# Eleven exponential tiles, a product in place and reordered ScalarE copies in an attention and feedforward kernel

## The chip, the cores and the metric

The kernel runs on one core of a Trainium2 chip. The metric is the device time of one execution in microseconds (us); lower is better. A core has five engines that run their own instruction queues in order: TensorE (PE in the profile, with its weight loads apart as PEld), VectorE (DVE), ScalarE (ACT), GpSimd (POOL) and SyncE (SP), which issues all the DMAs here. Semaphores make one engine wait for another.

## The reference

For x of 2048 tokens by 512, in float32:

```python
xn = layernorm(x)                                  # no gain, no bias
q, k, v = split(xn @ wqkv)                         # 32 heads of 16
p = softmax(q @ k.T * 16 ** -0.5)                  # 2048 x 2048 for each head
s = concat(p @ v) @ wo
h = (xn @ w_gate) * (xn @ w_up)                    # 2048 x 1792
g = silu(h @ w_down)
out = x + s * g
```

## The kernel before

**Attention in units and rounds.** The 32 heads are taken in 8 groups of four, and the queries in 4 chunks of 512: 32 units. A unit has 16 rounds of 128 keys, so there are 512 rounds, numbered `n` in the main loop (L863). In a round, for each of the four heads j, `expo` (L611) lets TensorE compute a transposed 128 x 512 score tile `t` with the maxima folded in as two more rows, and ScalarE takes the exponential of it into an SBUF tile `e`. Between them `score` (L587) computes, 21 rounds ahead (`LEAD`), a score tile `s` whose row maxima VectorE reduces (`mx`, L594); `maxima` (L596) turns these into the rows that a later unit subtracts.

**The value block.** In every even round, after its four `expo`, `values` (L848) first runs what has been put into `before_values`, and then `block` (L622): TensorE multiplies V with the eight `e` tiles of the two rounds before, four heads side by side in the columns of the array, into one PSUM bank `pv`. ScalarE copies it to `part` (L639; the first of a unit straight to `acc`, L634), and GpSimd adds `part` to `acc` (L640, recorded as L65, as is everything that GpSimd and SyncE issue through the helper there). `finish` (L642) normalises a finished unit with two VectorE transposes and stores it to DRAM.

**Rings.** `t` and `pv` share three PSUM banks (tag `st`) in the order of use: of the nine tiles in two rounds, `pv` comes last, the first `t` after it takes the bank that the third `t` of the even round had, the next `t` that of the fourth, and the third `t` that of `pv` itself. `s` has three banks, the tag `misc` of the filler two. The `e` tiles are a ring of ten (`EBUFS`), `part` a ring of two. When the third exponential of an even round is issued, eight tiles wait for the block and two more hold the round's first exponentials.

**The filler.** Between the heads' steps, in three of the four gaps of a round (`GAPS`), `Filler.part` emits matmuls of other work so that TensorE has something between scores: at first the projections of the next heads (`proj_pair`, 13 pairs), then the feedforward (`ffn`, L364), then the output (`ending`, L468). All of it is done in float32r with each operand split into a high and a low half and three terms. `pair` (L268) computes two results at once in the upper and the lower 64 rows of the array, in two halves; after the first half ScalarE reads one element of it (`look`, L289). A pair of the feedforward gives gate and up; ScalarE copies the gate out of PSUM to `g` (L392, one tile), VectorE multiplies it with up into `h` (L349, one tile), and GpSimd splits `h` into `hh` and `hl`. The copy stands in ScalarE's queue where the pair ends, the product waits in `before_values`. Down-projected results `y` are written or added up by `add` (L408), also in `before_values`. A finished chunk's `silu` (L352) gives four steps of tanh on ScalarE and two operations on GpSimd; `later` takes one step in the rounds with `kt % 4 == 2` (L887), after the round's fourth exponential. Weights are loaded whole and split by GpSimd some steps after (`soon`, L124).

**The end.** `ending` multiplies the heads' outputs, loaded back and split by `o_split` (L422), with `wo` (loaded and split in one go in L398), and `end` (L451) makes `x + s * g`: VectorE multiplies `z` in PSUM with the silu into SBUF (L458), and GpSimd, or late in the kernel VectorE (L459), adds x. For every second tile of the last chunk VectorE multiplies in PSUM (L454) and adds from there (L455).

**Order.** The program order is kept on TensorE, ScalarE and VectorE (`ORDERED`, L48). GpSimd's and SyncE's instructions are put in order by the framework's scheduler after the first 18 rounds, so that a change elsewhere can move them.

Of the kernel before, what the change touches and what calls it, by code (L numbers as in the profile page):

```python
# [11 lines left out]
F32 = mybir.dt.float32  # L12
F32R = mybir.dt.float32r
# [20 lines left out]
GAPS = [(0, 1, 2), (1, 2, 3)]  # L34
SLOTS = 24 * (NC * (NG // 2 - 1) + 1) + 36 * NF * NC
SPLIT_ROUNDS = 4
EBUFS = 10
PBUFS = 2
HBUFS = 2
QBUFS = 2  # L40
FINAL_AT = 8
# [9 lines left out]
def body(ctx, tc, x, wqkv, wo, wg, wu, wd, out):  # L51
# [23 lines left out]
    def dma(dst, src):  # L75
        sync.dma_start(dst, src)
# [72 lines left out]
    def etile():  # L149
        return ep.tile([P, 512], F32, name="e", bufs=EBUFS)  # L150

    def parts():
        return ep.tile([P, 512], F32, name="part", bufs=PBUFS)

    qkv = ExitStack()
    qp = qkv.enter_context(tc.tile_pool(name="qkv", bufs=1))
# [75 lines left out]
    def split_rows(raw, hi, lo):  # L232
        pool.tensor_copy(hi, raw)
        pool.tensor_tensor(lo, raw, hi, op=OP.subtract)
# [110 lines left out]

    later = []

    def product(h, u, g, hi, lo):
        nc.vector.tensor_tensor(h, u, g, op=OP.mult)  # L349
        split_rows(h, hi, lo)  # L350

    def silu(fp, c, y):  # L352
        for t in range(4):
# [12 lines left out]
    def ffn(nxt):  # L366
        fp = fst["fp"]
        for c in range(NC):
            if c == 0:
                fh, fl = xh[0], xl[0]  # L370
            else:
                fh, fl = [keep.tile([P, ND, 512], F32R, name=n) for n in ("fh", "fl")]
                dmar(fh, XD[c][0])
                dmar(fl, XD[c][1])
            y = fp.tile([P, 4, D], F32, name="y")
            for ti, fs in enumerate(THIRDS):
                hh = fp.tile([P, 5, 512], F32R, name="hh")
                hl = fp.tile([P, 5, 512], F32R, name="hl")
                dh = fp.tile([P, 5, D], F32R, name="dh")
                dl = fp.tile([P, 5, D], F32R, name="dl")  # L380
                for i, f in enumerate(fs):
                    ws = nxt
                    if not (c == NC - 1 and f == NF - 1):
                        nxt = gu_weights((f + 1) % NF)
                    raw = fp.tile([P, D], F32, name="wdr", bufs=2)
                    dma(raw, wd[f * P:(f + 1) * P])
                    soon(8, lambda raw=raw, i=i, dh=dh, dl=dl: split_rows(raw, dh[:, i], dl[:, i]))
                    outs = []
                    yield from pair(outs, [("misc", f"{n}{c}_{f}") for n in "gu"], [terms(lambda d: wh[:, d], lambda d: wl[:, d],
                                                 lambda d: fh[:, d], lambda d: fl[:, d], ND) for wh, wl in ws])  # L390
                    g = fp.tile([P, 512], F32, name="g", bufs=1)
                    nc.scalar.activation(g, outs[0], AF.Copy)  # L392
                    h = fp.tile([P, 512], F32, name="h", bufs=1)
                    before_values.append(lambda h=h, u=outs[1], g=g, hi=hh[:, i], lo=hl[:, i]: product(h, u, g, hi, lo))
                if c == NC - 1 and fs[-1] == NF - 1:
                    fst["y"] = y
                    fst["w"] = [keep.tile([P, ND, D], F32R, name=n) for n in ("fh", "fl")]
                    for d in range(ND):  # L398
                        raw = fp.tile([P, D], F32, name="wdr", bufs=2)
                        dma(raw, wo[d * P:(d + 1) * P])  # L400
                        split_rows(raw, *[t[:, d] for t in fst["w"]])
                for t in range(0, 4, 2):
                    outs = []
                    yield from pair(outs, [("misc", f"y{c}_{ti}_{u}") for u in (t, t + 1)], [terms(lambda i: hh[:, i, u * P:(u + 1) * P],
                                                 lambda i: hl[:, i, u * P:(u + 1) * P],
                                                 lambda i: dh[:, i], lambda i: dl[:, i], len(fs)) for u in (t, t + 1)])
                    for n, o in enumerate(outs):
                        def add(o=o, y=y[:, t + n], first=ti == 0, n=n):  # L408
                            if first and n:
                                nc.vector.tensor_copy(y, o)  # L410
                            elif first:
                                nc.scalar.activation(y, o, AF.Copy)
                            else:
                                nc.vector.tensor_tensor(y, o, y, op=OP.add)  # L414
                        before_values.append(add)
            later.append(silu(fp, c, y))


# [3 lines left out]
    def o_split(c, tiles):  # L422

        for d, (oh, ol) in enumerate(tiles):
            heads = 8 if c < NC - 1 or d < ND - 1 else 4
            n = heads * DH
            raw = (wtile(("w1r", "w0r")[d]).rearrange("p d q -> p (d q)") if d < 2 else
                   fst["fp"].tile([P, D], F32, name="wdr", bufs=2))
            dma(raw[:n], OD[c][8 * d:8 * d + heads, 0:DH])
            pool.tensor_copy(oh[:n], raw[:n])  # L430
            pool.tensor_tensor(ol[:n], raw[:n], oh[:n], op=OP.subtract)
        ops[c] = now[0], tiles

    def small_tiles():
# [15 lines left out]

    def end(c, t, o, yt, xt):  # L451
        tt = 4 * c + t
        if t % 2 and c == NC - 1:
            nc.vector.tensor_tensor(o, o, yt, op=OP.mult)  # L454
            nc.vector.tensor_tensor(yt, o, xt, op=OP.add)  # L455
        else:
            late = now[0] >= NU * 16 - LEAD and c < NC - 1
            nc.vector.tensor_tensor(yt, o, yt, op=OP.mult)  # L458
            (nc.vector if late else pool).tensor_tensor(yt, yt, xt, op=OP.add)  # L459
        dma(out[tt * P:(tt + 1) * P], yt)  # L460

    def o_terms(c, t):
# [80 lines left out]

    def last_heads():
        fp = fst["fp"]
        th = fp.tile([P, 512], F32, name="g", bufs=1).bitcast(F32R)
        tl = fp.tile([P, 512], F32, name="h", bufs=1).bitcast(F32R)
        nc.scalar.activation(th, fst["tn"], AF.Copy)
        nc.vector.tensor_tensor(tl, fst["tn"], th, op=OP.subtract)
        fst["t"] = th, tl  # L550
# [71 lines left out]
    def block(todo):  # L622

        i = todo[0][0]
        g = i // NC
        o = psum("st", f"pv{i}")
        for n, (_, kt, es) in enumerate(todo):
            for j in range(4):
                h0 = (4 * g + j) * VW
                nc.tensor.matmul(o[32 * j:32 * j + 32], V[:, kt, h0:h0 + 32], es[j],  # L630
                                 start=n == 0, stop=n == len(todo) - 1)
        if todo[0][1] == 0:
            sums[i] = keep.tile([P, 512], F32, name="acc", bufs=2)
            nc.scalar.activation(sums[i], o, AF.Copy)  # L634
        elif i >= NU - 2 and kt >= NT - 2:
            nc.vector.tensor_tensor(sums[i], o, sums[i], op=OP.add)
        else:
            part = parts()
            nc.scalar.activation(part, o, AF.Copy)  # L639
            pool.tensor_tensor(sums[i], sums[i], part, op=OP.add)  # L640

# [29 lines left out]
    def early():  # L671
# [5 lines left out]
        for which in (1, 0):  # L677
            wraw.append(wtile(f"w{which}r"))
            dma(wraw[-1], wqkv[:, which * D:which * D + P].rearrange("(d p) f -> p d f", p=P))
        norm["raws"] = raws = [etile() if d < 2 else parts() for d in range(ND)]  # L680
        for d in range(ND):
            dma(raws[d], wqkv[d * P:(d + 1) * P, 2 * D:])
        for tt in range(4, NT):
# [115 lines left out]
    def step_small(q):  # L799
        if q and next(q[0], 1):  # L800
            q.pop(0)
# [57 lines left out]
    with tc.manual_schedule(engines=ORDERED):  # L859
# [3 lines left out]
        for n in range(NU * 16):  # L863
            now[0] = n
            Tied.on = n < 18
            i, kt = divmod(n, 16)
            g, c = divmod(i, NC)
            si, sr = divmod(n + LEAD, 16)
            if kt == 8 and i + 2 < NU:
                load_q(i + 2)  # L870
            if kt == 0 and g + 1 < NG and c == 1:
                load_k(g + 1)
            es = []
            for j in range(4):
                es.append(expo(i, kt, j))
                if si < NU:
                    score(si, sr, j ^ 1)
                step()
                if j == 1:
                    prepare()  # L880
                if n and j in GAPS[n % 2]:
                    if fil.done:
                        fil = Filler(ending(), lambda n: 2)
                    fil.part(n % 2 and j == 1)
            if sr == 15 and si < NU:
                maxima(si, 8 if si < NU - 1 else 4)
            if kt % 4 == 2:  # L887
                step_small(later)
            if n == 0:
                run(fst["v"])  # L890
            elif n % 2 == 0 or n == NU * 16 - 1:
                values()
            prev.append((i, kt, es))
# [27 lines left out]
```

## Time and profile before

| | us |
|---|---|
| median of 3 runs | 1832.85 (1831.91 to 1835.38) |
| the profiled execution's own time | 1833.15 |
| its span, first to last instruction | 1831.4 |
| TensorE busy | 1784.9 |
| VectorE busy | 1479.7 |
| ScalarE busy | 1297.9 |
| GpSimd busy | 884.3 |

The mean granted TensorE clock was 0.995 of full speed. A line of the profile's groups gives the source line, the engine, the operation with its tiles (written `out<-in`), the shapes and the count; then the busy time, the mean duration of one in ns, and the engine's idle time ahead of them with what ended it. A line of waits gives who waited for whom, the sum in us, how often, and the longest. A line of a timeline gives the start in us, the duration, and the instruction, with the idle time ahead of it in brackets. A granted TensorE clock of 0.5 means half speed. Matmul ends are modelled, so starts are the better measure.

### The profile page before, as it was taken

The page shows a single profiled execution, that of the slowest core. Times are in us where ns is not written, and L with a number is a line of the kernel's source. Part 1 is how long each engine was busy: PE and PEld are TensorE (multiplying, and loading weights), DVE is VectorE, ACT ScalarE, POOL GpSimd, SP SyncE. Part 2 cuts the span into 40 slices and gives each one's busy share as a digit, 9 for nine tenths or more (in the row PEclk, how much of TensorE's full clock was granted, in tenths as well). Part 3 has the DMA queues.
Part 4 walks back from the last instruction along what each step waited for, and adds up shares of the span by engine and source line. Part 5 has one row for each costly group of instructions (what it writes and reads, how often), then busy time and mean ns, then how long its engine had stood idle before and what let it go on. Part 6 is the DMA issues. An engine that isn't in the chain of part 4 may idle for free.

```text
span 1831.4 us, 35270 instructions
## 1 busy us (share of the span) xinstructions
PE 1784.9 (97%) x13578; PEld 1074.6 (59%) x13578; DVE 1479.7 (81%) x2441; ACT 1297.9 (71%) x2575; POOL 884.3 (48%) x919
## 2 busy tenths in 40 slices
PE   9999999999999999999999999999999999999998
PEld 6655555555655555556656555655655556556554
DVE  6878888788888888888888888888888888888832
ACT  6257777677777777777777777777777777777765
POOL 5214444743644546455354653553546445355562
PEclk9999999999999999999999999999999999999999
DMA  5317523511231122311024210411135111011341
GB/s 200 98 44 219 219 97 124 146 39 39 62 74 51 61 77 67 74 50 51 28 62 111 73 56 28 97 50 39 42 96 113 40 51 51 27 53 55 115 136 69
DMA packets 117235, 145.79 MB, mean 80 GB/s; under 512 B 12620, under 2 KB 74060, under 8 KB 114380
## 3 DMA queue, kind: packets, MB, share of 16 engines
q1 hardware_dynamic: 117068, 143.55, 26.7%
q8 instruction: 106, 1.74, 0.4%
q14 instruction: 61, 0.50, 0.1%
HBM read 95.94 MB, written 47.45 MB: 78 GB/s over the span
## 4 chain that ended last, share of the span: by engine, by line
PE 88%; ACT 5%; issue 3%; POOL 2%; DMA 1%; DVE 1%; SPq 0%; ACTq 0%; POOLq 0%; DVEq 0%
PE pv L630 22%; PE t L617 20%; PE s L592 10%; PE g L285 5%; PE u L285 5%; PE y L281 4%; PE y L285 4%; PE g L281 4%; PE u L281 3%; ACT e L619 2%; PE p L285 2%; PE v L262 2%; PE p L281 2%; ACT g L392 1%; PE z L285 1%
## 5 line engine op out<-in xcount | busy, mean ns | idle before, releaser
L594 DVE TENSOR_REDUCE mx<-s 128x1 f32<-128x512 f32 x2048 | 1305.1, 685 | 209.3 <-PE s L592 163.2
L619 ACT ACTIVATE e<-t 128x512 f32<-128x512 f32 x2048 | 1121.9, 611 | 461.6 <-PE pv L630 410.8
L617 PE MATMUL t<-qs,ks 50*128 50x512 f32 x2048 | 846.9, 425 | 25.6 <-ACT e L619 24.6
L592 PE MATMUL s<-ks,qs 48*128 48x512 f32 x2048 | 835.1, 428 | 3.3 <-DVE mx L594 2.5
L617 PEld LDWEIGHTS t<-qs,ks 50*128 50x128 f32 x2048 | 377.9, 185 | 370.3 <-ACT e L619 282.6
L65 POOL TENSOR_TENSOR acc<-acc,part 128x512 f32<-128x512 f32 x222 | 286.4, 1290 | 465.4 <-ACT part L639 465.3
L630 PE MATMUL pv<-e,V 128*32 128x512 f32 x4096 | 492.5, 598 | 0.0
L592 PEld LDWEIGHTS s<-ks,qs 48*128 48x128 f32 x2048 | 368.8, 184 | 31.2 <-issue 6.1
L630 PEld LDWEIGHTS pv<-e,V 128*32 128x32 f32 x4096 | 107.1, 109 | 240.8 <-issue 216.3
L639 ACT ACTIVATE part<-pv 128x512 f32<-128x512 f32 x222 | 134.2, 604 | 0.8 <-POOL acc L65 0.7
L285 PE MATMUL u<-fh,w0h 64*128 64x512 f32 x224 | 90.3, 403 | 1.8 <-DVE h L349 1.8
L349 DVE TENSOR_TENSOR h<-u,g 128x512 f32<-128x512 f32 x56 | 38.7, 692 | 65.4 <-ACT g L392 62.1
L285 PE MATMUL y<-dh,hh 64*128 64x512 f32 x224 | 91.1, 407 | 0.1
L281 PE MATMUL u<-fh,w0h 64*128 64x512 f32 x224 | 90.6, 405 | 0.0
L285 PE MATMUL g<-fh,w1h 64*128 64x512 f32 x224 | 90.4, 404 | 0.0
L65 POOL CAST w0h<-w0r 128x512 fp32r<-128x512 f32 x60 | 36.6, 610 | 110.9 <-PE u L281 82.7
L281 PE MATMUL y<-dh,hh 64*128 64x512 f32 x224 | 89.3, 399 | 0.7 <-DVE y L414 0.7
L285 PE MATMUL u<-fl,w0h 64*128 64x512 f32 x224 | 88.5, 395 | 0.0
L285 PE MATMUL u<-fh,w0l 64*128 64x512 f32 x224 | 88.4, 395 | 0.0
L281 PE MATMUL g<-fh,w1h 64*128 64x512 f32 x224 | 88.4, 395 | 0.0
L281 PE MATMUL g<-fh,w1l 64*128 64x512 f32 x224 | 88.4, 394 | 0.0
L281 PE MATMUL g<-fl,w1h 64*128 64x512 f32 x224 | 88.2, 394 | 0.0
(261 smaller groups left out, 3093.6 us busy)
## 6 DMA issues: line engine op xcount, KB each, us to landing
w0r<-in_wu_dram SPq DMA_DIRECT2D x56, 256.0 KB
w1r<-in_wg_dram SPq DMA_DIRECT2D x56, 256.0 KB
wdr<-in_wd_dram SPq DMA_DIRECT2D x56, 256.0 KB
qs<-QD SPq DMA_DIRECT2D x64, 192.0 KB
ks<-KD SPq DMA_DIRECT2D x12, 768.0 KB
KD<-hl SPq DMA_DIRECT2D x16, 512.0 KB
QD<-hl SPq DMA_DIRECT2D x16, 512.0 KB
OD<-acc SPq DMA_DIRECT2D x31, 256.0 KB
```

Source lines behind the costliest of these rows:

```text
L65: got = getattr(self.engine, name)(*args, **kw)
L262: nc.tensor.matmul(o, l(d), r(d), start=k == d == 0, stop=k == 2 and d == ND - 1)
L281: nc.tensor.matmul(outs[k], l[LOWER], r[LOWER], start=k == 0 and n == 0, stop=(stop or k == 0) and n == len(low) - 1, skip_group_check=k == 1)
L285: nc.tensor.matmul(outs[1 - k], l[UPPER], r[UPPER], start=k == 0 and m == 0, stop=(stop or k == 0) and m == len(high) - 1, skip_group_chec ...
L349: nc.vector.tensor_tensor(h, u, g, op=OP.mult)
L392: nc.scalar.activation(g, outs[0], AF.Copy)
L592: nc.tensor.matmul(o, QS[i][b:b + KB, pr, t * P:(t + 1) * P], k[b:b + KB, pr, kc * 512:(kc + 1) * 512], start=True, stop=True)
L594: nc.vector.tensor_reduce(MX[i][:, j, t, kc:kc + 1], o, axis=AX.X, op=OP.max)
L617: nc.tensor.matmul(o, k[b:b + KR, pr, kt * P:(kt + 1) * P], QS[i][b:b + KR, pr], start=True, stop=True)
L619: nc.scalar.activation(e, o, AF.Exp, scale=DH ** -0.5)
L630: nc.tensor.matmul(o[32 * j:32 * j + 32], V[:, kt, h0:h0 + 32], es[j], start=n == 0, stop=n == len(todo) - 1)
L639: nc.scalar.activation(part, o, AF.Copy)
```

## The change

Six edits: the `e` tiles become eleven, and `part` has one buffer of its own and, once the feedforward's pool is open, a second one in that pool (`part2`), used in turn; the product of gate and up is written over the gate's copy `g`, of which there are now two, and `h` is gone; the `silu` step moves from behind the round's fourth exponential to ahead of it, and the first of the first third's two `y` copies is issued where its pair ends and no longer in `before_values`; the loads and splits of `wo` and the splits in `o_split` are spread over later steps; outputs of the last 21 rounds' range are multiplied in PSUM and added from there on VectorE. TensorE's order stays the same.

```diff
-EBUFS = 10
-PBUFS = 2
+EBUFS = 11
...
-    def parts():
-        return ep.tile([P, 512], F32, name="part", bufs=PBUFS)
+    turn = [0]
+
+    def part_tile():
+
+        turn[0] ^= 1
+        if turn[0] and "fp" in fst:
+            return fst["fp"].tile([P, 512], F32, name="part2", bufs=1)
+        return ep.tile([P, 512], F32, name="part", bufs=1)
...
-    def product(h, u, g, hi, lo):
-        nc.vector.tensor_tensor(h, u, g, op=OP.mult)
-        split_rows(h, hi, lo)
+    def product(u, g, hi, lo):
+        nc.vector.tensor_tensor(g, u, g, op=OP.mult)
+        split_rows(g, hi, lo)
...
-                    g = fp.tile([P, 512], F32, name="g", bufs=1)
+                    g = fp.tile([P, 512], F32, name="g", bufs=2)
                     nc.scalar.activation(g, outs[0], AF.Copy)
-                    h = fp.tile([P, 512], F32, name="h", bufs=1)
-                    before_values.append(lambda h=h, u=outs[1], g=g, hi=hh[:, i], lo=hl[:, i]: product(h, u, g, hi, lo))
+                    before_values.append(lambda u=outs[1], g=g, hi=hh[:, i], lo=hl[:, i]: product(u, g, hi, lo))
...
                     for d in range(ND):
-                        raw = fp.tile([P, D], F32, name="wdr", bufs=2)
-                        dma(raw, wo[d * P:(d + 1) * P])
-                        split_rows(raw, *[t[:, d] for t in fst["w"]])
+                        def wo_split(d=d, w=fst["w"]):
+                            raw = fp.tile([P, D], F32, name="wdr", bufs=2)
+                            dma(raw, wo[d * P:(d + 1) * P])
+                            soon(4, lambda: split_rows(raw, *[t[:, d] for t in w]))
+                        soon(5 * d + 4, wo_split)
...
-                        before_values.append(add)
+                        if ti == n == 0:
+                            add()
+                        else:
+                            before_values.append(add)
...
             dma(raw[:n], OD[c][8 * d:8 * d + heads, 0:DH])
-            pool.tensor_copy(oh[:n], raw[:n])
-            pool.tensor_tensor(ol[:n], raw[:n], oh[:n], op=OP.subtract)
+            soon(4 + 3 * d, lambda raw=raw[:n], oh=oh[:n], ol=ol[:n]: split_rows(raw, oh, ol))
...
-        if t % 2 and c == NC - 1:
+        if now[0] >= NU * 16 - LEAD and (t % 2 or c < NC - 1):
             nc.vector.tensor_tensor(o, o, yt, op=OP.mult)
             nc.vector.tensor_tensor(yt, o, xt, op=OP.add)
         else:
-            late = now[0] >= NU * 16 - LEAD and c < NC - 1
             nc.vector.tensor_tensor(yt, o, yt, op=OP.mult)
-            (nc.vector if late else pool).tensor_tensor(yt, yt, xt, op=OP.add)
+            pool.tensor_tensor(yt, yt, xt, op=OP.add)
...
-            part = parts()
+            part = part_tile()
...
-        norm["raws"] = raws = [etile() if d < 2 else parts() for d in range(ND)]
+        norm["raws"] = raws = [etile() if d < 3 else part_tile() for d in range(ND)]
...
             for j in range(4):
+                if j == 3 and kt % 4 == 2:
+                    step_small(later)
                 es.append(expo(i, kt, j))
...
-            if kt % 4 == 2:
-                step_small(later)
```

More of the change, by code (lines that the diff above doesn't have):

```diff
@@ L545, in last_heads @@
         fp = fst["fp"]
-        th = fp.tile([P, 512], F32, name="g", bufs=1).bitcast(F32R)
-        tl = fp.tile([P, 512], F32, name="h", bufs=1).bitcast(F32R)
+        th, tl = [fp.tile([P, 512], F32, name="g", bufs=2).bitcast(F32R) for _ in range(2)]
         nc.scalar.activation(th, fst["tn"], AF.Copy)
```

## The prediction

> **What bounds the kernel now.** I read the page first: span and busy times, then the chain, then the two costliest groups.
>
> ```profile
> span 1831.4 us, 35270 instructions
> ...
> PE 1784.9 (97%) x13578; PEld 1074.6 (59%) x13578; DVE 1479.7 (81%) x2441; ACT 1297.9 (71%) x2575; POOL 884.3 (48%) x919
> ...
> PE 88%; ACT 5%; issue 3%; POOL 2%; DMA 1%; DVE 1%; SPq 0%; ACTq 0%; POOLq 0%; DVEq 0%
> ...
> L594 DVE TENSOR_REDUCE mx<-s 128x1 f32<-128x512 f32 x2048 | 1305.1, 685 | 209.3 <-PE s L592 163.2
> L619 ACT ACTIVATE e<-t 128x512 f32<-128x512 f32 x2048 | 1121.9, 611 | 461.6 <-PE pv L630 410.8
> ```
>
> TensorE carries the chain, and looks full. But a matmul's record runs on while its weights are late, so busy time is no proof; the waits are. They are the second view:
>
> ```profile
> ACT e L619 <- PE pv L630: 410.8, 255, 1.9
> PEld t L617 <- ACT e L619: 282.6, 610, 0.8
> DVE h L349 <- ACT g L392: 62.1, 55, 1.5
> PEld t L617 <- ACT look L289: 44.4, 53, 0.8
> PEld t L617 <- ACT part L639: 15.9, 64, 0.6
> ```
>
> In 255 of the 256 value blocks ScalarE idles until the block's matmuls give it a free `e` tile, and behind that the weight load of a score matmul waits for an exponential. The third view, timelines of TensorE and ScalarE around blocks, gives the price. A plain block:
>
> ```profile
> 916.21 1.92 PE L630 MATMUL pv<-e,V 128*32 128x512 f32 x16
> 918.06 0.49 PE L617 MATMUL t<-qs,ks 50*128 50x512 f32 x1
> ...
> 918.43 0.50 PE L617 MATMUL t<-qs,ks 50*128 50x512 f32 x1
> ...
> 918.76 0.39 PE L285 MATMUL u<-fh,w0h 64*128 64x512 f32 x1
> ```
> ```profile
> 917.29 1.09 ACT L619 ACTIVATE e<-t 128x512 f32<-128x512 f32 x2 [1.54 <-PE pv L630]
> 918.26 0.61 ACT L634 ACTIVATE acc<-pv 128x512 f32<-128x512 f32 x1
> ```
>
> The block begins at 916.21. Only at 917.29, 1.08 later, can the third and fourth exponentials of the round run. The first `t` behind the block uses the third's bank and is in time; the second `t` uses the fourth's, and comes at 918.43, 0.37 behind the first; the next pair follows 0.33 later. And a block where ScalarE has a copy to make between the two exponentials:
>
> ```profile
> 1430.23 0.49 PE L617 MATMUL t<-qs,ks 50*128 50x512 f32 x1
> ...
> 1431.08 0.50 PE L617 MATMUL t<-qs,ks 50*128 50x512 f32 x1 [0.35 <-ACT e L619]
> ...
> 1431.42 0.39 PE L285 MATMUL u<-fh,w0h 64*128 64x512 f32 x1
> ...
> 1431.66 0.39 PE L285 MATMUL u<-fl,w0h 64*128 64x512 f32 x1
> ```
> ```profile
> 1429.45 0.60 ACT L619 ACTIVATE e<-t 128x512 f32<-128x512 f32 x1 [1.30 <-PE pv L630]
> 1429.95 0.59 ACT L392 ACTIVATE g<-g 128x512 f32<-128x512 f32 x1
> 1430.42 0.60 ACT L619 ACTIVATE e<-t 128x512 f32<-128x512 f32 x1
> 1430.90 0.62 ACT L639 ACTIVATE part<-pv 128x512 f32<-128x512 f32 x1
> ```
>
> Here 0.85 lies between the two `t`. The rhythm: a pair behind one whose weights were loaded late follows at 0.34 (1431.08 to 1431.42), any other at 0.24 (1431.42 to 1431.66).
>
> [...]
>
> **The change part by part.** *Eleven tiles.* When the third exponential of an even round is issued, eight tiles wait for the block and two hold the round's first exponentials. With eleven it finds one free; only the fourth waits for the block, 1.08 into it. At 0.60 it ends 1.68 into it. The first `t` comes at 1.85 (918.06 less 916.21), so the second `t` can have its weights loaded behind it, at 0.34, with the next pair at 0.24. Copies and `look` fall before the fourth exponential, into the wait. Which blocks gain what: the copies are counted by
>
> ```profile
> L392 ACT ACTIVATE g<-g 128x512 f32<-128x512 f32 x56 | 33.2, 592 | 0.0
> L318 ACT ACTIVATE qr<-p 128x512 f32<-128x512 f32 x13 | 7.7, 592 | 0.0
> ```
>
> - Copy blocks, 56 + 13 = 69: (0.85 - 0.34) + (0.34 - 0.24) = 0.61 each, 42.1.
> - `look` blocks, 53 by the waits' row: one of them is
>
> ```profile
> 1437.58 0.49 PE L617 MATMUL t<-qs,ks 50*128 50x512 f32 x1
> ...
> 1437.97 0.49 PE L617 MATMUL t<-qs,ks 50*128 50x512 f32 x1
> ...
> 1438.31 0.40 PE L285 MATMUL g<-fh,w1h 64*128 64x512 f32 x1
> ```
>
>   (0.39 - 0.34) + (0.34 - 0.24) = 0.15, together 8.0.
> - Plain blocks, 255 - 69 - 53 = 133: (0.37 - 0.34) + (0.33 - 0.24) = 0.12. Where TensorE later waits for the exponentials that queue behind the block's copy, only what the copy gains counts: it starts at 918.26 and the block's matmuls end at 918.13 (916.21 + 1.92), so 0.13 at most less a signal's delay. I take 0.09 to 0.12, 0.10: 13.3 (12.0 to 16.0).
>
> Sum 63.4. What hides the third exponential is ScalarE's idle 1.3 to 1.5 ahead of the block's release; if that cover were gone the gain would be too.
>
> *Product in place, two `g`.* VectorE's 692 ns product is the same work. Once, the old `h` cost TensorE time: VectorE could not overwrite it until GpSimd had read it.
>
> ```profile
> 356.28 0.39 PE L281 MATMUL g<-fh,w1h 64*128 64x512 f32 x1
> 358.46 0.59 PE L285 MATMUL u<-fh,w0h 64*128 64x512 f32 x1 [1.80 <-DVE h L349]
> ```
> ```profile
> 357.00:362.00 5.00, 3.54 (x18) 2.79 (x20) 3.27 (x5) 2.27 (x5) 5.00 (x6) 0.67 0.03 7
> ```
>
> The gap is 2.18 where 0.24 is normal, 1.94. Behind it the granted clock was 0.67 in a 5 us stretch: with only full and half speed, 0.33 x 2 x 5 = 3.3 us at half, which costs 1.7. Now VectorE writes into the tile that ScalarE just filled and waits for no reader. 3.6 gained. The `g` copy waits for the split of two products back instead; that is far off.
>
> *The silu step ahead of the fourth exponential.* Tanh used to run between the fourth exponential and the copy of `pv`, so that the third `t` waited for that copy:
>
> ```profile
> 678.58 0.50 PE L617 MATMUL t<-qs,ks 50*128 50x512 f32 x1 [0.21 <-ACT part L639]
> ```
>
> The row of waits for `part` sums to 15.9 in 64 cases, but these overlap other work. Sixteen steps at most, 0.2 to 0.4 each: 3 to 6; I take 4, and let the `y` copies, which save one wait and may delay an exponential, cost 1 of it. 3.
>
> *`part`: a cost.* In the first stage `part` has one buffer. A copy must then wait for GpSimd's addition of the one before. 27 copies lie there (the row below, for 0 to 320 us), and one pair of them overlaps:
>
> ```profile
> L639 ACT ACTIVATE part<-pv 128x512 f32<-128x512 f32 x27 | 16.3, 605 | 0.0
> ```
> ```profile
> 195.84 0.61 ACT L639 ACTIVATE part<-pv 128x512 f32<-128x512 f32 x1
> ```
> ```profile
> 197.75 1.28 POOL L65 TENSOR_TENSOR acc<-acc,part 128x512 f32<-128x512 f32 x1
> ```
>
> The addition of the part before ends at 199.03, held up by weight splits on GpSimd, so this copy waits 3.19. Queued behind it on ScalarE are all the next exponentials, and the third `t` waits for its bank: TensorE stops about 3.2. A shorter stop, the 2.18 above, was followed by 3.3 us of half clock; so 1.7 more, and -4.9. If the clock stays up it is -3.2; if a second copy meets the same, -9.8.
>
> [...]
>
> *The late multiply in PSUM.* Before, the addition took two SBUF operands, and one of them ran beside GpSimd's additions:
>
> ```profile
> 1751.86 3.94 DVE L459 TENSOR_TENSOR hh<-hh 128x512 f32<-128x512 f32 x1
> 1755.72 0.68 DVE L458 TENSOR_TENSOR hh<-z,hh 128x512 f32<-128x512 f32 x1
> ```
>
> That is 3.94 where the product from PSUM behind it takes 0.68, so up to 3.3 is saved. Against it: the PSUM bank is held for a second operation of about 0.7, and GpSimd's new order puts a silu step ahead of the small `mm` that VectorE waits for first:
>
> ```profile
> 1750.96 0.61 POOL L65 TENSOR_SCALAR e<-e 128x512 f32<-128x512 f32 x1
> ...
> 1752.77 1.25 POOL L65 TENSOR_TENSOR y<-e,y 128x512 f32<-128x512 f32 x1
> ```
>
> That is 1.86 more of waiting, less what an earlier tanh gives back. Net +1; from -2, where the order costs most, to +5, where TensorE's stop goes and no half clock follows it.
>
> [...]
>
> *Spread splits of `wo`.* The product's split no longer queues behind them; the `mm` behind them comes about when it did. 0, between -2 and +2.
>
> Sum: 63.4 + 3.6 + 3 - 4.9 + 1 + 0 = 66.1. From the execution's own 1833.15 that leaves 1767.0; the median of the runs is 0.3 lower. **I predict 1767 us.**
>
> **The rivals.**
>
> *TensorE's busy time is real.* Then no more than 1831.4 - 1784.9 = 46.5 can go: 1787 at best. For it: 97%. Against: the starts 0.85 apart in the copy blocks.
>
> *ScalarE's chain takes over.* Behind each block come the copy of `pv` and six exponentials before the next block can have its bank. If that chain already sets the pace, plain and `look` blocks gain nothing and copy blocks only the copy's 0.48 (1430.90 less 1430.42): 69 x 0.48 = 33, with the other terms 36: 1797. Against it: ScalarE is 71% busy. VectorE is less of a danger: eight reductions of 0.685 are 5.5 a block, where a block takes 1831.4 / 256 = 7.2 and would take 6.9; and it loses its 62.1 of waiting for `g`.
>
> *The eleventh tile frees nothing*, because the ring turns otherwise than I count and the third exponential still waits: 1833.15 - 3.6 - 3 + 4.9 - 1 = 1830.5, no measurable change (0.2% of the time, 3.7, is about what a measurement can tell).
>
> *Slower: the single `part`.* If GpSimd is late not for one copy of the first stage but for many, each costs 4.9. All 27 would cost 132, so 1833.15 - 71 + 132 = 1894. It decides from 71 / 4.9, some 15 copies on. Against it: only one pair overlaps in the trace of before, and the new order leaves the same operations ahead of most additions.
>
> **How the numbers follow.** My forecast has 0.67; TensorE's busy time 0.10; ScalarE's chain 0.15; no eleventh tile 0.03; the single `part` 0.05. Faster by over 0.2%: 0.92, within 0.2%: 0.03, slower: 0.05. The forecast's own range, with plain blocks at both ends, two stalled parts, and the end at -2 and +5, is 1757 to 1778; with the two rivals on its upper side, 1754 to 1798.
>
> **What would show it.** The wait of ScalarE for `pv` falls from about 1.6 to about 1 each and only the fourth exponential has it; the second `t` behind a block follows at 0.34 in copy blocks too; VectorE's wait for `g` falls below 20; the 2.18 gap behind `h` is gone; one new wait of `part` for `acc` of some 3 us stands near 190 us, with half clock behind it; no VectorE addition takes over 1 us at the end. I am wrong if the copy blocks keep starts over 0.5 apart, or if new waits of `part` for `acc` sum to over 20.

## The result, and the profile after

The changed kernel takes 1776.76 us (median, 1775.57 to 1776.99) beside 1833.34 us of the kernel before on the same chip: ratio 0.969, 95% interval 0.967 to 0.971. The profiled execution took 1776.67, 56.5 less than before; forecast were 66.1 less.

The page after:

```profile
span 1774.9 us, 35053 instructions
...
PE 1743.9 (98%) x13578; PEld 1054.0 (59%) x13578; DVE 1446.6 (82%) x2441; ACT 1331.5 (75%) x2575; POOL 888.9 (50%) x919
...
PE 94%; POOL 2%; issue 1%; ACT 1%; DVE 1%; DMA 1%; POOLq 0%; SPq 0%; ACTq 0%; DVEq 0%
...
L600 DVE TENSOR_REDUCE mx<-s 128x1 f32<-128x512 f32 x2048 | 1276.3, 683 | 249.2 <-PE s L598 174.0
L625 ACT ACTIVATE e<-t 128x512 f32<-128x512 f32 x2048 | 1112.6, 603 | 266.7 <-PE pv L636 205.1
```

TensorE's busy time fell by 41.0 with the same 13578 matmuls: so part of what the records call busy had been waiting, for weights by the rows below; the mean record of a `t` matmul went from 425 to 415 ns. ScalarE's share of the chain went from 5% to 1%. The waits:

```profile
PEld t L623 <- ACT e L625: 244.8, 410, 0.8
ACT e L625 <- PE pv L636: 205.1, 248, 1.2
...
PEld pv L636 <- ACT e L625: 38.1, 112, 0.4
...
PEld t L623 <- ACT part L645: 29.2, 56, 7.8
...
ACT part L645 <- DMA QD<-hl: 8.1, 1, 8.1
...
ACT part L645 <- POOL acc L64: 5.8, 3, 4.1
```

ScalarE's wait for the block halved: 205.1 / 248 = 0.83 each, where it was 1.61. The third row was 24.5 before: blocks now wait more for exponentials. The fifth, a wait for a DMA, is new, and nothing in the prediction answers to it.

A block with the copy of `g`, on TensorE and on ScalarE (the same block of the kernel, counted from the first, as the prediction's at 1430):

```profile
1387.64 0.49 PE L623 MATMUL t<-qs,ks 50*128 50x512 f32 x1
...
1387.97 0.40 PE L623 MATMUL t<-qs,ks 50*128 50x512 f32 x1
1388.21 0.39 PE L286 MATMUL g<-fh,w1h 64*128 64x512 f32 x1
...
1388.44 0.39 PE L286 MATMUL g<-fl,w1h 64*128 64x512 f32 x1
```
```profile
1385.75 0.63 ACT L397 ACTIVATE g<-g 128x512 f32<-128x512 f32 x1
1386.87 0.60 ACT L625 ACTIVATE e<-t 128x512 f32<-128x512 f32 x1 [0.49 <-PE pv L636]
1387.83 0.60 ACT L645 ACTIVATE part<-pv 128x512 f32<-128x512 f32 x1 [0.37 <-PE pv L636]
```

The copy of `g` now lies ahead of the fourth exponential, in the wait, and the second `t` comes 0.33 behind the first where it was 0.85 behind. The next pair follows at 0.24. And a plain block that gained nothing (6.00 before, 5.98 now; the last line is cut off by the end of the view, and its block has sixteen matmuls like the others):

```profile
970.33 1.92 PE L636 MATMUL pv<-e,V 128*32 128x512 f32 x16
972.18 0.50 PE L623 MATMUL t<-qs,ks 50*128 50x512 f32 x1
...
972.52 0.40 PE L623 MATMUL t<-qs,ks 50*128 50x512 f32 x1
...
976.31 1.07 PE L636 MATMUL pv<-e,V 128*32 128x512 f32 x8
```
```profile
972.38 0.60 ACT L645 ACTIVATE part<-pv 128x512 f32<-128x512 f32 x1 [0.37 <-PE pv L636]
972.87 3.56 ACT L625 ACTIVATE e<-t 128x512 f32<-128x512 f32 x7
```

Its second `t` is early too, at 0.34. But ScalarE can copy `pv` only when the block's matmuls have ended, 2.05 into the block as before (918.26 less 916.21 there), and from then on it works without a pause: seven exponentials up to 976.43. The next block begins at 976.31, 5.98 behind the last. The other blocks that gained nothing were not followed one by one.

Where the 56.5 came from, by the time from the first `pv` matmul of a block to that of the next, before less after (blocks counted from 0):

```
copy blocks, without 31 and 36         67 blocks   45.5
look blocks                            53           9.9
plain blocks, without 12 and the last 132          10.3   (83 of them 0.0)
block 36, a copy block (gap behind h gone)          4.5
block 12, a plain block                            -4.7
block 31, a copy block                             -8.6
ahead of the first block, and from the last on     -0.4
```

Block 31 is the new stop, at the switch from the projections to the feedforward. First ScalarE, then the chain through it in order of time (start, us, what):

```profile
317.66 0.60 ACT L625 ACTIVATE e<-t 128x512 f32<-128x512 f32 x1 [0.58 <-PE pv L636]
326.32 0.60 ACT L645 ACTIVATE part<-pv 128x512 f32<-128x512 f32 x1 [8.06 <-DMA QD<-hl]
```
```profile
318.66 3.57 POOL hl L64 x4
322.24 0.33 SPq L64
322.62 3.44 DMA QD<-hl
326.32 0.61 ACT part L645
326.97 0.79 PE t L623
```
```profile
326.97 0.79 PE L623 MATMUL t<-qs,ks 50*128 50x512 f32 x1 [7.32 <-ACT part L645]
```
```profile
323.00:332.00 9.00, 5.03 (x30) 3.79 (x34) 3.00 (x5) 4.24 (x8) 2.93 (x4) 0.62 1.07 278
```

ScalarE's first copy into `part2` waits until the last projection's halves `hl` have been made by GpSimd and stored. Then TensorE, idle for 7.32, goes on at half clock: the 0.62 of these 9 us is (1 - 0.62) x 2 x 9 = 6.8 us at half speed. By the trace's clock records they run from 323.8 to 330.6, so that some 3 of them fall into the stop itself and cost nothing more.

### The profile page after: what moved, and what is told of

The parts are those of the page before. It is cut to its first block, busy times and chain, and to the rows that moved or that the text cites. A ratio compares the mean times of both kernels' runs of the same rounds, so it can differ in the third digit from the quotient of the medians.

```text
span 1774.9 us, 35053 instructions
## 1 busy us (share of the span) xinstructions
PE 1743.9 (98%) x13578; PEld 1054.0 (59%) x13578; DVE 1446.6 (82%) x2441; ACT 1331.5 (75%) x2575; POOL 888.9 (50%) x919
## 4 chain that ended last, share of the span: by engine, by line
PE 94%; POOL 2%; issue 1%; ACT 1%; DVE 1%; DMA 1%; POOLq 0%; SPq 0%; ACTq 0%; DVEq 0%
PE pv L636 26%; PE t L623 19%; PE s L598 12%; PE u L286 6%; PE g L286 6%; PE y L286 4%; PE y L290 4%; PE u L290 3%; PE g L290 3%; PE p L286 3%; PE v L267 2%; PE z L286 1%; PE p L290 1%; PE z L290 1%; PE p L267 1%
## 5 line engine op out<-in xcount | busy, mean ns | idle before, releaser
L600 DVE TENSOR_REDUCE mx<-s 128x1 f32<-128x512 f32 x2048 | 1276.3, 683 | 249.2 <-PE s L598 174.0
L625 ACT ACTIVATE e<-t 128x512 f32<-128x512 f32 x2048 | 1112.6, 603 | 266.7 <-PE pv L636 205.1
L623 PE MATMUL t<-qs,ks 50*128 50x512 f32 x2048 | 804.8, 415 | 11.3 <-ACT part L645 10.9
L598 PE MATMUL s<-ks,qs 48*128 48x512 f32 x2048 | 798.8, 421 | 2.1 <-DVE mx L600 2.1
L623 PEld LDWEIGHTS t<-qs,ks 50*128 50x128 f32 x2048 | 360.2, 185 | 314.4 <-ACT e L625 244.8
L598 PEld LDWEIGHTS s<-ks,qs 48*128 48x128 f32 x2048 | 351.1, 185 | 34.1 <-DVE mx L600 5.8
L290 PE MATMUL u<-fh,w0l 64*128 64x512 f32 x224 | 88.5, 395 | 0.0
L286 PE MATMUL u<-fh,w0l 64*128 64x512 f32 x224 | 88.1, 393 | 0.0
```

Source lines behind the costliest of these rows:

```text
L286: nc.tensor.matmul(outs[k], l[LOWER], r[LOWER], start=k == 0 and n == 0, stop=(stop or k == 0) and n == len(low) - 1, skip_group_check=k == 1)
L290: nc.tensor.matmul(outs[1 - k], l[UPPER], r[UPPER], start=k == 0 and m == 0, stop=(stop or k == 0) and m == len(high) - 1, skip_group_chec ...
L598: nc.tensor.matmul(o, QS[i][b:b + KB, pr, t * P:(t + 1) * P], k[b:b + KB, pr, kc * 512:(kc + 1) * 512], start=True, stop=True)
L600: nc.vector.tensor_reduce(MX[i][:, j, t, kc:kc + 1], o, axis=AX.X, op=OP.max)
L623: nc.tensor.matmul(o, k[b:b + KR, pr, kt * P:(kt + 1) * P], QS[i][b:b + KR, pr], start=True, stop=True)
L625: nc.scalar.activation(e, o, AF.Exp, scale=DH ** -0.5)
```

## The experiments

Each is the changed kernel with the edit shown, except the first, which is the kernel before. All were compared with the kernel before on their own chip, whose median lay between 1832.5 and 1833.1.

**The tiles alone**, with one `part` and, in the feedforward's pool, `part2`.

```diff
-EBUFS = 10
-PBUFS = 2
+EBUFS = 11
...
-            part = parts()
+            part = part_tile()
...
-raws = [etile() if d < 2 else parts() for d in range(ND)]
+raws = [etile() if d < 3 else part_tile() for d in range(ND)]
```

> Only the eleven tiles, with the ring of one `part` (and `part2` in the feedforward stage) that makes room for them; product, silu step, output copies, splits and late multiply as before. Theory (the eleventh tile frees the third exponential, and that carries the gain): blocks gain 63 to 66, the two stops that come with the ring of `part` cost 4.7 and 8.6 as in the changed kernel, the 2.18 gap behind `h` stays: 1833 - 64 + 13 = 1782 us (1779 to 1786). Rival (the new order, silu ahead of the fourth exponential and the output copies ahead of the matmuls, carries a good part of the gain): over 1795.

Measured: 1780.67 us, ratio 0.971 (0.970 to 0.973). The theory holds: copy blocks gain 45.7, `look` blocks 9.9, plain ones 7.6, and blocks 12 and 31 lose 4.9 and 8.5. In the 7.6 stands a loss of 2.4 in block 237; the other plain ones gain 10.0, where the changed kernel has 9.3 without that block. One thing was not expected: block 36 gains its 4.5 here too, with the old `h`.

**The old ring.**

```diff
-EBUFS = 11
+EBUFS = 10
+PBUFS = 2
...
-        turn[0] ^= 1
-        if turn[0] and "fp" in fst:
-            return fst["fp"].tile([P, 512], F32, name="part2", bufs=1)
-        return ep.tile([P, 512], F32, name="part", bufs=1)
+        return ep.tile([P, 512], F32, name="part", bufs=PBUFS)
...
-        norm["raws"] = raws = [etile() if d < 3 else part_tile() for d in range(ND)]
+        norm["raws"] = raws = [etile() if d < 2 else part_tile() for d in range(ND)]
```

> The changed kernel with the old ring: ten tiles for exponentials and two buffers of `part` throughout; product, order, splits and late multiply stay changed. Theory (the tiles carry nearly all): the gain of the blocks goes (66 to 67 by the traces) and the stops of `part` at 190 and 317 us go with it (13.4): 1776.8 + 66.5 - 13.4 = 1830 us (1826 to 1833). Rival (the new order carries a good part of it): under 1815.

Measured: 1827.15 us, 0.997 (0.996 to 0.998). Two of the waits on which the prediction rests are those of before:

```profile
ACT e L623 <- PE pv L634: 410.9, 255, 1.9
...
PEld t L621 <- ACT look L292: 44.4, 53, 0.8
```

So the rest of the change is worth 5.7 by itself with ten tiles, and the eleventh tile with its ring some 50 more. By blocks the 5.7 is the sum of three gains and many small losses: block 36 takes 6.7 in place of 10.6 (the gap behind `h` is gone), block 245 takes 7.3 in place of 13.0 (a stop at the end is gone), block 237 gains 1.4, and all else gives back some 4. Twelve of the sixteen blocks with a tanh step are 0.2 longer than before.

Ten tiles with the changed ring of `part` gave no time, since that program deadlocks; so the eleventh tile was not measured apart from its ring.

**The second `part` later.**

```diff
-        if turn[0] and "fp" in fst:
+        if turn[0] and "fp" in fst and now[0] >= 68:
```

> The changed kernel, but the second buffer `part2` is used from round 68 on, two blocks later. Theory (at the switch to the feedforward stage the copy waited 8.1 us because part2 lies in memory of `hl` that the store of QD was still reading): no wait there, 1777 - 8.6 = 1768 us (1767 to 1770), block 31 takes 6.7 in place of 15.3. Rival (GpSimd, busy with splits until 323, would have held the copies anyhow): the stop moves to the next copy, 1772 to 1777.

Measured: 1769.0 us, 0.965 (0.964 to 0.967). The copy of block 31 now waits for the block alone:

```profile
318.37 0.60 ACT L645 ACTIVATE part<-pv 128x512 f32<-128x512 f32 x1 [0.37 <-PE pv L636]
```

Block 31 takes 6.0 in place of 15.3. GpSimd makes the same splits, so the stop was not theirs but a matter of memory: `part2` had been given a place where `hl` still had to be read by its store. The run gains 7.8 and not 9.3, since block 36 and others give some back.

**A single `part` throughout.**

```diff
-        if turn[0] and "fp" in fst:
+        if False:
```

> The changed kernel with a single `part` throughout, no `part2`. In the trace of the changed kernel nine copies of the later stages start before the addition of the copy ahead of them has ended, by 17.3 us in all (most of it from 1642 to 1697). Theory (each such overlap becomes a stop, some with half clock behind, and the stop of 8.6 at the switch goes): 1777 - 8.6 + 17 + 4 = 1789 us (1778 to 1796). Rival (a single `part` stalls most copies): over 1830.

Measured: 1784.34 us, 0.973 (0.972 to 0.975).

```profile
ACT part L645 <- POOL acc L64: 26.2, 12, 5.3
```

Twelve copies wait, not most of them. Without its own stop at the switch `part2` is worth 1784.3 - 1769.0 = 15.3.

**The old product**, with one `g` and an `h` of its own.

```diff
-        nc.vector.tensor_tensor(g, u, g, op=OP.mult)
-        split_rows(g, hi, lo)
+        nc.vector.tensor_tensor(h, u, g, op=OP.mult)
+        split_rows(h, hi, lo)
...
-                    g = fp.tile([P, 512], F32, name="g", bufs=2)
+                    g = fp.tile([P, 512], F32, name="g", bufs=1)
...
+                    h = fp.tile([P, 512], F32, name="h", bufs=1)
...
```

> The changed kernel with the product in a tile `h` of its own and one `g`, as before. Theory (the product in place took the 2.18 us gap behind `h` away): the gap and the half clock behind it come back: 1777 + 4.5 = 1781 us. Rival (with eleven tiles the gap does not arise, since the kernel with the tiles alone and the old `h` shows 6.05 us for that block too): 1776 to 1778.

Measured: 1777.08 us, 0.970 (0.968 to 0.971), the same as the changed kernel. The theory falls: with the rest of the change in place the product over `g` gains nothing (block 36 takes 6.0 here too). Why, the next run asks.

**The old product and `part2` later**, both edits above.

> `part2` from round 68 on, and the product in a tile `h` of its own as before. Theory (the stop of 8.6 us at the switch let GpSimd catch up, and that is why the old `h` cost nothing with eleven tiles; without the stop the gap behind `h` returns): 1769 + 4 = 1773 us. Rival (the blocks' new rhythm alone keeps GpSimd ahead): 1769 us, as with the product in place.

Measured: 1769.86 us, 0.966 (0.964 to 0.967). VectorE's wait is back, and half clock behind it:

```profile
350.98 0.69 DVE L354 TENSOR_TENSOR h<-u,g 128x512 f32<-128x512 f32 x1 [1.43 <-POOL hl L64]
```
```profile
350.00:358.00 8.00, 7.02 (x42) 4.54 (x42) 5.25 (x9) 4.47 (x9) 7.84 (x10) 0.79 0.22 63
```

Block 36 takes 9.3, and 6.7 with `part2` late and the product over `g`. So it was the long stop in block 31 that kept the wait behind `h` away, by giving GpSimd time to catch up. The wait is shown; its price in the whole is not, since the medians differ by 0.9 and the intervals overlap.

**The old order of ScalarE's copies.**

```diff
-                if j == 3 and kt % 4 == 2:
-                    step_small(later)
...
+            if kt % 4 == 2:
+                step_small(later)
...
-                        if ti == n == 0:
-                            add()
-                        else:
-                            before_values.append(add)
+                        before_values.append(add)
```

> The changed kernel with the silu step behind the round's fourth exponential and all copies of `y` ahead of the next block, as before. Theory (sixteen steps, 0.2 to 0.4 each, less 1 for the `y` copies): 3 us lost, 1780 us (1778 to 1782). Rival (with eleven tiles the third exponential is early enough to hide tanh anyway): no difference, 1776 to 1778.

Measured: 1775.02 us, 0.968 (0.967 to 0.970): no loss, rather a gain of 1.7, though the intervals overlap. Its trace is 2.8 shorter in block 245 and about 1.7 longer in all others together. What is longer lies in blocks 12, 13 and 31 (1.9), ahead of the first tanh at 664, where this edit changes nothing. The sixteen blocks that hold a tanh in the kernel before have gained nearly the same, 10.4 here and 10.7 in the changed kernel. The 3 of the prediction isn't there. Block 245 is shorter because GpSimd makes the small `mm` ahead of the silu step here, as in the kernel before, and VectorE waits 7.2 for it and not 9.6.

**The old end.**

```diff
-        if now[0] >= NU * 16 - LEAD and (t % 2 or c < NC - 1):
+        if t % 2 and c == NC - 1:
...
+            (nc.vector if late else pool).tensor_tensor(yt, yt, xt, op=OP.add)
```

> The changed kernel with the late multiply and addition as before (product from PSUM into SBUF, then an addition of two SBUF operands on VectorE). Theory (net +1 of the change): 1778 us, with one VectorE addition of over 3 us beside GpSimd's additions; range 1775 to 1782. Rival (all of the 3.3 of that addition was on the path): 1780 or more.

Measured: 1776.24 us, 0.969 (0.968 to 0.970): no difference. VectorE's additions of two SBUF operands:

```profile
L467 DVE TENSOR_TENSOR dl<-dl 128x512 f32<-128x512 f32 x4 | 3.9, 983 | 0.1
L467 DVE TENSOR_TENSOR hh<-hh 128x512 f32<-128x512 f32 x4 | 3.3, 831 | 0.1
```

The longest takes 1.63, so that the 3.94 of before does not come back, and this run can't tell what it cost. TensorE's stop in block 245 is nearly unchanged by the edit (13.2 for 13.4), so it has another cause in the changed kernel:

```profile
DVE mt L611 <- POOL mm L64: 9.6, 1, 9.6
PEld z L286 <- DVE hh L463: 4.4, 1, 4.4
```
```profile
1699.00:1707.00 8.00, 6.01 (x29) 4.44 (x30) 2.65 (x5) 2.38 (x5) 2.31 (x2) 0.57 0.60 203
```

VectorE waits 9.6 for the small `mm` of the last unit at the end of GpSimd's queue, the late products stand behind it, and TensorE stops and goes on at half clock (0.57). Ahead of `mm` GpSimd now has the silu step's two operations, of which this is the second:

```profile
1697.38 1.26 POOL L64 TENSOR_TENSOR y<-e,y 128x512 f32<-128x512 f32 x1
1698.61 0.22 POOL L64 TENSOR_TENSOR mm<-m,mm 128x16 fp32r<-128x16 f32 x1
```

In the kernel before, `mm` came first, and TensorE's stop of the same length ended with the product that stands right behind the 3.94:

```profile
PE z L285 <- DVE hh L458: 4.1, 1, 4.1
```

With the tiles alone both are found again, an addition of 3.94 and a stop of 4.1. So the late multiply takes one cause of the stop away and the silu step's place brings another. With the old ring, which has the late multiply and `mm` ahead of the silu step, the stop is gone. No run takes the late multiply alone out of that one.

The next runs try to repair the three stops.

**Block 11 added by VectorE.** The block ahead of the stop in block 12 has its sum made straight from PSUM.

```diff
-        elif i >= NU - 2 and kt >= NT - 2:
+        elif i >= NU - 2 and kt >= NT - 2 or now[0] == 24:
             nc.vector.tensor_tensor(sums[i], o, sums[i], op=OP.add)
```

> The changed kernel, with the result of one value block (block 11, the one ahead of the stop at 190 us) added to `acc` by VectorE straight from PSUM, so that its `part` copy and GpSimd's addition go. Theory (block 12's copy waited 4.1 us for that addition only): block 12 takes 6.3 in place of 11.0, 1777 - 4.7 = 1772 us. Rival (GpSimd is behind there for more than one block, the stop moves on): 1775 to 1777.

Measured: **1764.27 us, 0.963 (0.961 to 0.964)**, the fastest of all, and 12.5 under the changed kernel where 4.7 were expected. Block 12 takes 6.3 in place of 11.0, as forecast. But block 31 lost its 9.3 too: with one copy less the turn of `part` and `part2` falls the other way, and block 31's copy goes to `part`. The stop of block 31 hung on the parity of a counter. A wait of 2.1 for `part` in block 36 gave 1.7 back.

**`mm` on VectorE**, for all 32 units.

```diff
-        pool.tensor_tensor(mm[:, :, 1], m, mm[:, :, 0], op=OP.subtract)
+        nc.vector.tensor_tensor(mm[:, :, 1], m, mm[:, :, 0], op=OP.subtract)
```

> The changed kernel, with the small subtraction `mm` made by VectorE in place of GpSimd. Theory (the stop of 6 us at 1696 with half clock behind it comes from VectorE waiting 9.6 us for `mm`, which stood behind nine splits and additions in GpSimd's queue): block 245 takes about 6 in place of 13.45, 1777 - 7 = 1770 us (1768 to 1772). Rival (the products wait for the loads or for the split of the attention's result anyhow): 1774 to 1777.

Measured: 1783.79 us, 0.973 (0.972 to 0.974), 7 slower. Block 245 takes 6.8 in place of 13.4, as the theory has it. But the subtraction is dear on VectorE. Its group here, and then the changed kernel's on GpSimd:

```profile
L607 DVE TENSOR_TENSOR mm<-m,mm 128x16 fp32r<-128x16 f32 x32 | 19.4, 606 | 1.1
```
```profile
L64 POOL TENSOR_TENSOR mm<-m,mm 128x16 fp32r<-128x16 f32 x32 | 7.2, 224 | 63.0 <-DVE mm L606 63.0
```

Where a product comes right behind it, that is late by as much, and TensorE waits; eight of the blocks at which a unit's `mm` is made are 1.0 to 1.2 longer:

```profile
412.29 1.21 DVE L607 TENSOR_TENSOR mm<-m,mm 128x16 fp32r<-128x16 f32 x1
413.42 0.68 DVE L354 TENSOR_TENSOR g<-u,g 128x512 f32<-128x512 f32 x1
```
```profile
414.15 0.50 PE L290 MATMUL y<-dh,hh 64*128 64x512 f32 x1 [0.77 <-DVE g L354]
```

**The three repairs together** (`part2` from round 68, block 11 on VectorE, all `mm` on VectorE).

> The changed kernel with three repairs: `part2` from round 68 on, block 11 added by VectorE, `mm` on VectorE. Theory (three stops in different places, so their prices add): 1777 - 7.7 - 4.7 - 7 = 1757.5 us (1755 to 1761). Rival (taking one stop away lets GpSimd fall behind elsewhere): 1762 to 1768.

Measured: 1768.26 us, 0.965 (0.963 to 0.966). By blocks, 4.6, 9.3 and 6.8 are gained at blocks 12, 31 and 245, but the moved `mm` costs some 10 in the blocks at which it is made, which the expectation had not counted.

**Blocks 11 and 35 on VectorE, and the last `mm` alone.**

```diff
-        elif i >= NU - 2 and kt >= NT - 2:
+        elif i >= NU - 2 and kt >= NT - 2 or now[0] in (24, 72):
...
-        pool.tensor_tensor(mm[:, :, 1], m, mm[:, :, 0], op=OP.subtract)
+        (nc.vector if i == NU - 1 else pool).tensor_tensor(mm[:, :, 1], m, mm[:, :, 0], op=OP.subtract)
```

> The changed kernel with VectorE adding blocks 11 and 35 to `acc` straight from PSUM, and making `mm` for the last unit alone. Theory: the stops at 190 and 317 us go as in the run with block 11 alone (1764.3), block 36 loses its wait of 2.1 us for `part` (1.5), block 245 its 6.7, and the other maxima do not pay for a subtraction of two SBUF operands on VectorE (1.2 each at 13 places when all were moved): 1764.3 - 6.7 - 1.5 = 1756 us (1754 to 1759). Rival (without the stop at 245 GpSimd's queue holds the next block): 1760 to 1764.

Measured: 1767.64 us, 0.964 (0.963 to 0.966); the expectation was wrong. Block 245 gains 6.8 and block 36 1.7, but block 35 takes 17.3 in place of 6.7:

```profile
347.65 0.69 DVE L642 TENSOR_TENSOR acc<-pv,acc 128x512 f32<-128x512 f32 x1 [9.65 <-POOL acc L64]
```

VectorE's addition into `acc` has to wait for GpSimd's addition of the block before, which stands behind nine others in its queue. At block 11 GpSimd had been up to date. Blocks 246, 249 and what follows the start of the last give back 2.5 of block 245's gain. Block 11 with the last `mm` but without block 35 wasn't tried.

## Why the prediction was right

The forecast was faster by 66.1 with a range from 1754 to 1798; the size came out 56.5. Its main step held and one step was missing. That 1776.76 lies even in the forecast's own range, up to 1778, is partly luck: that end allowed for a second stop of `part`, but behind GpSimd's additions and at 4.9, and the one that came has another cause and cost 8.6.

- **Eleven tiles: right.** Forecast 63.4, found 45.5 + 9.9 + 10.3 = 65.7 in the blocks, and the run with the tiles alone shows 45.7, 9.9 and, without block 237, 10.0. The 65.7 holds also what the copies, the end and the splits did; forecast with them were 67.4. Copy blocks gave 0.68 each (0.61 forecast), `look` blocks 0.19 (0.15). *Plain blocks* were mis-sized: 0.08 for 0.10 on the mean, but as 83 blocks with nothing, 4 that lost 0.2 to 0.5, and 45 that gained, most of them 0.1 and more. In the block of the 83 that is shown above, the rival "ScalarE's chain takes over" is right: the copy begins 2.05 into the block before and after, and ScalarE has no pause behind it. The bound "0.13 at most less a signal's delay" was to be read as 0 there, for with eleven tiles too the copy starts 0.13 behind the block's end (972.38, where 970.33 + 1.92 = 972.25).
- **Product in place: right with ten tiles, but not a term to add.** Forecast 3.6. With the old ring block 36 loses its gap and 3.8 us, as forecast. In the changed kernel the block gained 4.5, but with the old product it gains them as well: the wait was GpSimd's backlog at that moment, and the new stop in block 31 took the backlog away. With that stop gone the wait came back, at 1.43.
- **Silu step and `y` copies: wrong.** Forecast 3, found none (1775.0 without them). The step that failed is "0.2 to 0.4 each" for sixteen steps: the blocks with a tanh gain the same with and without the edit, and with ten tiles twelve of them lose 0.2. The wait of 0.21 that the prediction shows was read as a price, and removing it freed nothing. Why not is not shown; with ten tiles tanh then stands between the two late exponentials, where the prediction itself has a copy cost time.
- **Single `part`: right as far as it went.** One copy, 4.1 of wait and 3.4 us of half clock behind it: 4.7 of loss, forecast 4.9, on the forecast's "near 190 us".
- **What was missing: the second `part`'s memory.** The step "one pair of copies overlaps, so one new wait" looked at the buffers of `part` alone. `part2` lies in the pool that opens when the projections' pool closes, and its first copy waited 8.06 for the store from `hl`. That cost 8.6 and is nearly the whole of the miss of 9.6; the other errors, of up to 3 in single terms, nearly cancel. The trace of before would have told it, by SyncE's last store from `hl` and block 31's copy:

```profile
326.95 0.32 SPq L65 DMA_DIRECT2D QD<-hl  x1
```
```profile
322.52 0.62 ACT L639 ACTIVATE part<-pv 128x512 f32<-128x512 f32 x1
```

  The store is issued 4.4 after the copy begins.
- **The late multiply: +1 forecast, -0.5 found in block 245 (13.4 for 13.0), as a sum of two that nearly cancel.** The 3.94 was on the path: with the old ring the stop behind it goes and the block takes 7.3. The price, the silu step ahead of `mm`, which the prediction put at 1.86 "less what an earlier tanh gives back", was too small: VectorE's wait for `mm` is 9.6 where it was 6.8, and the stop is back. With the old order of the copies the block takes 10.6.
- **Splits of `wo`: 0 forecast, not tried apart.** Block 237 takes 8.4 in the kernel before, 10.8 with the tiles alone, which has the old splits, and 7.4 with the whole change; with the tiles alone VectorE waits there 2.2 for `mm` in GpSimd's queue, so the spread may be worth some 3 with eleven tiles.
- **The busy time of TensorE** was no bound, as argued: 41.0 of it went, and the kernel gained 56.5 where that rival allows 46.5.

What was to show it: the starts at 0.34, the wait of under 1 and the one new wait near 190 are there; VectorE's wait for `g` is gone from the list; the additions at the end are down to 0.69. New waits of `part` for `acc` sum to 5.8, far under 20.

## What to carry to other kernels

When a buffer is moved into another pool, ask what lay in that memory and who reads it last: here the first write of `part2` waited 8.06 for the DMA of a store, ScalarE's exponentials behind the write waited with it, and TensorE was idle for 7.32. A stop caused by a backlog elsewhere belongs to the moment and not to the line that shows it; price an edit against such a stop only with the rest of the change in place, for it may vanish, as the wait behind `h` in block 36 did with the stop of 8.06 in block 31, and come back, as it did at 1.43 without that stop. Two edits that act on the same stop can hide each other: with one of them taken out nothing may change (1777.08 with the old product, 1776.76 without), so look at the block itself, in more than one run, before calling either worthless. And an operation moved to another engine to shorten a queue can delay what stands behind it there, as the `mm` of 1.21 on VectorE did with a product for which TensorE then idled 0.77, and can still wait for the old queue through a tile that it shares with it, as VectorE's addition into `acc` did for 9.65.

## What the hardware showed beside

- **VectorE beside GpSimd.** A subtraction of two SBUF operands of only 128 x 16 took VectorE 1.21 us (0.61 on the mean) where GpSimd takes 0.22 for it. It began at 412.29 and ended at 413.50, with this one of GpSimd's, which ends at 413.47:

```profile
412.18 1.29 POOL L64 TENSOR_TENSOR w1l<-w1r,w1h 128x512 fp32r<-128x512 f32 x1
```

  No run shows whether the one waited for the other.
- **The clock after short gaps.** In the clock records of the kernel before and of the changed kernel, half clock comes in stretches of 3.4 or 6.8 us, but for the last of each, 3.5 and 5.8, in which the run ends. In the run with blocks 11 and 35 on VectorE, whose TensorE waits 8.2 for the addition of block 35, the windows have 0.72 from 337 to 355, (1 - 0.72) x 2 x 18 = 10.1 of half clock. Gaps are given here from the start of one matmul to that of the next. In the run with the tiles alone TensorE has one of 2.1 (1641.98 to 1644.10), and 3.4 us of half clock follow ((1 - 0.79) x 2 x 8):

```profile
1641.00:1649.00 8.00, 6.18 (x37) 3.94 (x31) 4.43 (x9) 3.81 (x7) 4.56 (x5) 0.79 0.09 27
```

  In the run with block 11 on VectorE one of 1.8 (346.72 to 348.52) is followed by full speed:

```profile
344.00:352.00 8.00, 6.61 (x56) 3.72 (x58) 6.02 (x12) 5.26 (x11) 7.84 (x9) 1.00 0.23 68
```

  But the old product with `part2` late has 0.79 behind a gap of 1.0 (350.76 to 351.72) and a second one close to it, from 352.06 to past 352.6, so the length of one gap isn't all that decides. What does stays open.
